# A later place for the exp(k)·v product in the planned order, and a shorter sum-by-sum group at the end of a single block's output product

## The chip, the cores and the metric

The kernel runs on one core of a Trainium2 chip, as one launch. The metric is the device time of the whole program in microseconds (us). TensorE (PE) multiplies, VectorE (DVE) and ScalarE (ACT) do the elementwise work, GpSimd (POOL) helps a little, and SyncE (SP) issues nearly all DMAs. Each engine works through its own instructions in program order; an instruction that waits holds up those behind it on the same engine.

## The reference, cut to what matters

A linear attention feeds two gated expert layers.

```python
q_s = softmax(q, axis=feature);  k_s = softmax(k, axis=sequence)
kv  = k_s.T @ v                  # per batch and head, 64 x 64
x   = q_s @ kv                   # 4608 rows x 512
g, val = x @ w_gate, x @ w_val   # 512 -> 1536
y   = (silu(g) * val) @ w_out    # 1536 -> 512
h   = max(y @ w1, y @ w2, y @ w3)  # 512 -> 768
out = h @ w_out2                 # 768 -> 512
```

There are 8 batches of 8 heads with 576 rows each. All is float32; the kernel splits an operand into a high and a low part in a rounded type (`..h`, `..l`, `hhi`, `hlo`) and adds three products for one.

## The kernel before, in words

The 4608 rows are worked in nine pieces of 512, in six blocks: pieces 0, 1 and 2 singly ("single blocks", `plan_one`), then three pairs (`plan`), which use a seven-product scheme for 2x2 pieces (`wino_unit`). A block runs the G and V products (gate and value, 12 features of 128 columns), the O output product over those 12 features (F1), then the W1, W2, W3 products (6 features, F2), and the P output product over those 6.

**One weight product** (`product`, L668) is six matmuls of 512 columns. A single block's `unit` has four of them, a pair's `wino_unit` seven. **One output feature** (`outs`, L684) is twelve matmuls: four sums e = 0..3, one for each 128 columns of the result (for P: rows), each with three matmuls into its own bank `acc0`..`acc3`. Most features run one after the other ("feature by feature"): all four sums of one feature, then the next. The last ones of a block run "sum by sum" (`emajor`): sum 0 over all features of the group, then sum 1, and so on, so that the first banks are finished early and their readers (`y_plain`, which splits y into the operands b11 and b21 of W1, or `rows_out`, which copies the result rows) start before the last bank is done. A feature needs its hidden values (`hhi`, `hlo`, made by ACT at L719 and DVE at L723 from the last gated product) and its weights (`ow`, in three buffers; in blocks 0 and 1 made by ACT at L581 and DVE at L584, later loaded).

**The attention of the rows to come** runs beside this, in three chains of steps: one for k and v (`k_steps`), two for q (`q_steps`). For each batch and half of its heads the k chain loads, takes the maximum (DVE, POOL), subtracts it (L204, L209), takes exp in three pieces on ACT (`k_exp`, L218: two of `k`, one of the rest `kr`), multiplies exp(k) by v on PE (`kv_mm`, L270, 40 short matmuls into `pkv`), scales (L373 to L383) and splits into `kvhi`, `kvlo`. The q chains end in the products x = q·kv (`x_mm`, L433 to L435). The loads of the next k, its rest and v (L140) overwrite buffers that the product reads, and so stand behind it. The two runs of batch 0 stand in a hand-written prologue; fourteen runs go through the chain.

**The order** of all instructions is made before the launch by a planner written in the kernel: a walk over the PE's items with a planned clock (`clock[0]`), a planned calendar for ACT, DVE, POOL and SP (`do`, `gap`), and fixed costs. Each engine then gets its instructions in the order of planned times; on the chip only semaphores hold them to it. A chain step with kind "P" (a PE step) is put in at a slot: ahead of a weight product, when the planned clock has reached the chain's own time:

```python
if ch["steps"] and ch["steps"][0][0] == "P" and ch["t"] <= clock[0]:
```

Single blocks have a slot ahead of every weight product, pairs only ahead of products 0, 1, 5 and 6 of a `wino_unit`; output features have none, but for a pair's O features 6 to 8 of its second half. The exp steps have planned costs of 1.95, 0.65 and 0.42 us:

```python
steps += [("A", (1.95, 0.65, 0.42)[i], lambda c=c, t=t, i=i: k_exp(t, c, i)) for i in range(3)]
```

The 1.95 holds one ACT table load; an exp that follows a Silu has another table to load again, and so has the Silu after it (L704, planned at 0.62).

Of the kernel before, what the change touches and what calls it, by code (L numbers as in the profile page):

```python
# [21 lines left out]
def linear_attention_moe_moe_kernel(  # L22
# [738 lines left out]
    HALF = {"A": 0.42, "D": 0.43, "G": 0.85}  # L761
    ENG = {"D": nc.vector, "G": nc.gpsimd, "A": None}
    DVE_LATE = 1.0
    G_FIRST = False
    LATER = {3: (1, "P", 0), 4: (2, "O", 0)}
    events = []
# [17 lines left out]
    def gap(e, t, dur):  # L784
        b = busy[e]
        i = bisect.bisect_left(b, (t, t))
        if i and b[i - 1][1] > t:
            t = b[i - 1][1]
        while i < len(b) and b[i][0] < t + dur:
            t = max(t, b[i][1])  # L790
            i += 1
        return t, i
# [11 lines left out]
    def best(t, cost, fn, *a, engines="DG", by=0.0):  # L804

        if G_FIRST and not alone[0] and gap("G", t, cost["G"])[0] + cost["G"] < by:
            return do("G", t, cost["G"], fn, *a, nc.gpsimd)
# [5 lines left out]
    def sync(t, fn, *a):  # L813

        return do("S", t, 0.45, fn, *a) - LAT
# [4 lines left out]
    def take(t):  # L820

        i = min((i for i in range(NT_) if spare[i] is not None), key=lambda i: (max(spare[i], t), -spare[i]))
        t, spare[i] = max(t, spare[i]), None
        return t, i
# [96 lines left out]
    def advance(ch):  # L921
        off = 0.45 * (ch is chains[1]) / 1.8
        while ch["steps"] and ch["steps"][0][0] != "P" and (ch["t"] <= clock[0] + LOOK[len(marks) - 1] or ch.get("bank")):
            e, dur, fn = ch["steps"][0]
            if e == "gate":
                if fn not in gates:
                    return
                ch["t"] = max(ch["t"], gates[fn])
            elif e == "there":
                there[fn] = ch["t"]  # L930
            elif e == "bank":
                bank_free[ch["bank"]] = max(bank_free.get(ch["bank"], 0.0), ch["t"])
                ch["bank"] = None
            elif e == "open":
                gates[fn] = ch["t"]
            elif e == "load":
                t = max(ch["t"], ch.get("last", 0.0))
                for a in fn[1]:
                    t = (math.ceil(t / dur - off) + off) * dur
                    t = max(t + 0.01, sync(t, a))  # L940
                ch["last"] = t
                ch["loaded", fn[0]] = t + 4.5
            elif e == "loaded":
                ch["t"] = max(ch["t"], ch["loaded", fn])
            elif e == "B":
                ch["t"] = best(ch["t"], {"D": dur, "G": 2.0 * dur}, fn)
            elif e in ("D+", "D="):
                t, ch["i"] = take(ch["t"])
                ch["t"] = do("D", t, dur, fn, ch["i"])
            else:  # L950
                ch["t"] = do(e[0], ch["t"], dur, fn)
            if e in ("D-", "D="):
                drop(ch["i"], ch["t"])
            if DEBUG:
                log.append((round(clock[0], 1), chains.index(ch), e, round(ch["t"], 1)))
            ch["steps"].pop(0)
# [16 lines left out]
    def k_steps(runs, n_buf):  # L973

        steps = []
        loads = [k_loads(kbuf[n % n_buf], *run) for n, run in enumerate(runs)]

        def load(n, part):
            if n < len(runs):
                steps.append(("load", 1.8 if n == 0 else 1.0, ((n, part), loads[n][4:] if part else loads[n][:4])))  # L980

        load(0, 0)
        load(0, 1)
        for n, (j, hf) in enumerate(runs):
            c, t = {}, kbuf[n % n_buf]
            if j in LATER:
                steps.append(("gate", 0.0, ("later", j)))
            if n_buf == 2:
                load(n + 1, 0)
            steps.append(("loaded", 0.0, (n, 0)))  # L990
            steps.append(("D=", 1.15, lambda i, c=c, t=t: k_max(t, c, i)))
            steps.append(("loaded", 0.0, (n, 1)))
            steps += [("D", 0.42, lambda c=c, t=t: k_max_rest(t, c)), ("G", 1.4, lambda c=c: k_max_all(c))]
            steps += [("B", (1.22, 0.42)[i], lambda e, c=c, t=t, i=i: k_sub(t, c, i, e)) for i in range(2)]
            steps += [("A", (1.95, 0.65, 0.42)[i], lambda c=c, t=t, i=i: k_exp(t, c, i)) for i in range(3)]

            def kv(bank, c=c, t=t):
                for g in range(HP):
                    kv_mm(t, c, g, bank)

            steps.append(("P", 1.25, kv))
            steps += [("D", 1.1, lambda c=c, t=t: kv_scale(t, c)), ("bank", 0.0, None)]
            if n_buf == 1:
                load(n + 1, 0)
            load(n + 1, 1)
            steps += [("gate", 0.0, ("x", j - 2, hf))] * (j > 2) + [
                ("A", 0.6, lambda c=c, j=j, hf=hf: kv_hi(c, j, hf)),
                ("D", 0.4, lambda c=c, j=j, hf=hf: kv_lo(c, j, hf)),
            ]
            steps.append(("open", 0.0, ("kv", j, hf)))  # L1010
        return steps
# [63 lines left out]
    def conv_job(use, i):  # L1075
# [7 lines left out]
        a0, a1 = gap("A", t, 1.34)[0] + 1.34, gap("A", t, 0.68)[0] + 0.68  # L1083
        dve = gap("D", a1 + LAT, 1.81)[0] + 1.81 + DVE_LATE < gap("D", a0 + LAT, 1.39)[0] + 1.39
        t = do("A", t, 0.68 if dve else 1.34, conv_act, i, dve, o)
# [426 lines left out]
    for n, kinds, out_ in ((F1, ("G", "V"), "O"), (F2, ("W1", "W2", "W3"), "P")):  # L1512
        for p in range(n // 2):
            for i, kind in enumerate(kinds):
                flow.append((kind, p))
                f = 2 * p - 2 + i
# [69 lines left out]
    def plan_one(s):  # L1586

        how = ("conv", "plain")[s] if s < 2 else "parts"
        pair = s + 1 < NS and len(BLOCKS[s + 1]) == 2

        def start():
            if s == 0:
                chains[:] = [{"t": clock[0], "steps": []} for _ in range(3)]
                gates["kv", 0, 0] = gates["kv", 0, 1] = 0.0
                next_k(1)
            have["home"] = clock[0]
            if s == 0:
                gates["rows",] = clock[0]
                at(clock[0], new_rows)
            if s < 2:  # L1600
                at(clock[0], own_qt)

        mark(start)
        n = 0
        if pair:
            x = [lambda n=n: x_wino(n) for n in range(7)]
        for kind, f in flow:
            for j, when in LATER.items():
                if when == (s, kind, f):
                    mark(lambda j=j: gates.__setitem__(("later", j), clock[0]))  # L1610
            if kind in "OP":
                nf = F1 if kind == "O" else F2
                if f < nf - 3:
                    outs(s, kind, [f], 0, nf, how)
                elif f == nf - 3:
                    outs(s, kind, list(range(f, nf)), 0, nf, how, True, {nf - 1: ("s01", "s11")} if s > 1 else None, done=y_plain(0) if kind == "O" else rows_out(BLOCKS[s][0]))
                if (kind, f) == ("P", F2 - 4) and s + 1 < NS:
                    for i in (4, 5, 6) if pair else ():
                        mark(x[i])
                continue  # L1620
            if (kind, f) == ("G", 1) and s + 1 < NS:
                mark(lambda: begin_x(s + 1))
            if s == 0 and (kind, f) in (("G", 0), ("V", 0)):
                unit(0, kind, f, (0,), "conv", (1,), ("b0", "b0", "b2", "b2") if kind == "G" else ("b1", "b1", "b3", "b3"))
            else:
                b = [("b0", "b2", "b1")[(n + i) % 3] for i in range(2)]
                unit(s, kind, f, (0,), how, (0, 1), (b[0], b[0], b[1], b[1]), (kind, f) == ("W1", 0))
                n += 2
            if (s, kind) in MADE_IN:
                keys = [(s, kind, f, 0, i) for i in range(2)]  # L1630
                ahead("made", 8.0, made_job, keys, kind, f)
            if f == F2 // 2 - 1 and kind in ("W1", "W2", "W3") and s + 1 < NS:
                if kind == "W1":
                    mark(lambda: after(s))
                    if pair:
                        mark(x[1])
                elif kind == "W2" and pair:
                    mark(x[2])
                    mark(x[3])
                elif kind == "W3":  # L1640
                    if pair:
                        mark(x[0])
                    else:
                        mark(lambda: x_plain(BLOCKS[s + 1][0], 0))
                        mark(lambda: x_plain(BLOCKS[s + 1][0], 1))
# [209 lines left out]
```

## Time and profile before

| | |
|---|---|
| median of 3 runs | 1601.89 us (1601.54 to 1603.42) |
| the profiled execution's own time | 1603.53 us |
| its span, first to last instruction | 1601.7 us |
| PE busy | 1494.6 us, 93% of the span |
| DVE busy | 1035.5 us, 65% |
| ACT busy | 684.7 us, 43% |
| mean granted PE clock | 0.974 |
| chain that ended last: PE | 74% of the span |

The span is what the profiler saw between the first and the last instruction. A row of waits names who waited, for whom, the total in us, how often, and the longest. A row of a timeline gives start, duration, engine, line, operation and tiles, and in brackets the idle time ahead of it and what ended it. A row of windows gives a stretch, its length, then for each engine busy us and instruction count, then the granted PE clock (1.00 is full speed, 0.50 half).

### The profile page before, as it was taken

What the parts mean: (1) busy time and instruction counts of PE and PEld (TensorE: products, weight loads), DVE (VectorE), ACT (ScalarE), POOL (GpSimd) and SP (SyncE); (2) the same over time, 40 slices, a digit from 0 to 9 for tenths busy, and PEclk for the clock granted to TensorE, in tenths of its full rate; (3) what the DMA queues carried; (4) which work ended last, traced back from release to release, by engine and by line L of the source; (5) the groups of instructions that cost most, each with busy time, mean ns of one, the idle gap of its engine ahead of it and who ended that gap; (6) DMA issues with size and microseconds to landing.
All of it is one profiled execution on the core that took longest, in us unless ns stands there. A gap on an engine that the chain in (4) does not pass through costs nothing.

```text
span 1601.7 us, 20645 instructions
## 1 busy us (share of the span) xinstructions
PE 1494.6 (93%) x6946; PEld 1212.5 (76%) x6946; DVE 1035.5 (65%) x1789; ACT 684.7 (43%) x1184; POOL 98.2 (6%) x86
## 2 busy tenths in 40 slices
PE   3988899899999998989999999999999999999999
PEld 2666777688787886877777877888878878887787
DVE  7879985576867566566549885464388754444643
ACT  3778664643456435453453335432332342224212
POOL 1000000000000001002012130000010200000000
PEclk9999999899999998999999999999999999999999
DMA  6799685866687697886567757875666576646664
GB/s 184 205 316 288 191 238 159 234 196 187 179 268 253 230 321 228 254 247 203 170 214 236 233 178 249 229 207 161 223 181 184 175 233 195 202 139 218 202 187 161
DMA packets 302024, 342.71 MB, mean 214 GB/s; under 512 B 157536, under 2 KB 181088, under 8 KB 301920
## 3 DMA queue, kind: packets, MB, share of 16 engines
q1 hardware_dynamic: 297120, 340.22, 69.1%
q10 hardware_dynamic: 4800, 1.18, 0.4%
q8 instruction: 56, 0.92, 0.2%
q14 instruction: 48, 0.39, 0.1%
HBM read 257.16 MB, written 84.15 MB: 213 GB/s over the span
## 4 chain that ended last, share of the span: by engine, by line
PE 74%; DVE 9%; ACT 6%; DMA 5%; issue 3%; SPq 2%; POOL 0%; DVEq 0%; ACTq 0%; POOLq 0%
PE pb L668 48%; PE pacc L684 15%; PE pb L684 8%; PE pkv L270 1%; DMA ow<-parts_O 1%; DVE tall L738 1%; ACT L704 1%; SPq L156 1%; DVE hlo L723 1%; DMA v_sb<-in_v_dram 1%; ACT L218 1%; PE px L433 1%; DMA wino_G<-wall 1%; ACT plain L527 1%; ACT s L704 1%
## 5 line engine op out<-in xcount | busy, mean ns | idle before, releaser
L738 DVE TENSOR_TENSOR tall<-tall,pb 128x512 f32<-128x512 f32 x234 | 159.5, 683 | 192.2 <-PE pb L668 188.8
L668 PE MATMUL pb<-b11h,wall 128*128 128x512 f32 x756 | 271.6, 401 | 11.1 <-ACT s L704 6.2
L668 PE MATMUL pb<-b21h,wall 128*128 128x512 f32 x756 | 265.2, 393 | 0.0
L684 PE MATMUL pacc<-hhi,ow 128*128 128x512 f32 x576 | 192.8, 398 | 8.4 <-ACT hhi L719 7.2
L668 PEld LDWEIGHTS pb<-b11h,wall 128*128 128x128 f32 x756 | 144.4, 191 | 46.8 <-ACT s L704 8.0
L668 PEld LDWEIGHTS pb<-b21h,wall 128*128 128x128 f32 x756 | 143.3, 190 | 30.4 <-ACT tall L728 0.4
L728 ACT COPY tall<-pb 128x512 f32<-128x512 f32 x112 | 65.7, 587 | 215.1 <-PE pb L668 214.9
L668 PE MATMUL pb<-b11l,wall 128*128 128x512 f32 x378 | 150.1, 397 | 0.9 <-DVE b11l L455 0.9
L668 PE MATMUL pb<-b21l,wall 128*128 128x512 f32 x378 | 148.4, 393 | 1.0 <-DVE b21l L455 1.0
L684 PEld LDWEIGHTS pacc<-hhi,ow 128*128 128x128 f32 x576 | 110.3, 192 | 34.9 <-ACT hhi L719 9.4
L719 ACT CAST hhi<-tall 128x512 fp32r<-128x512 f32 x108 | 66.6, 618 | 150.3 <-DVE tall L713 111.1
L684 PE MATMUL pacc<-hlo,ow 128*128 128x512 f32 x288 | 114.7, 398 | 7.3 <-DVE hlo L723 7.3
L567 DVE TENSOR_TENSOR wall<-plain,wall 128x512 fp32r<-128x512 f32 x126 | 86.1, 686 | 36.2 <-ACT wall L564 36.0
L723 DVE TENSOR_TENSOR hlo<-tall,hhi 128x512 fp32r<-128x512 f32 x104 | 73.6, 708 | 46.3 <-ACT hhi L719 45.8
L684 PE MATMUL pacc<-ow,hhi 128*128 128x512 f32 x288 | 93.4, 406 | 6.5 <-DVE ow L584 6.1
L564 ACT CAST wall<-plain 128x512 fp32r<-128x512 f32 x126 | 76.8, 617 | 51.3 <-PE pb L668 16.2
L684 PE MATMUL pb<-hhi,ow 128*128 128x512 f32 x288 | 91.3, 392 | 1.4 <-DMA ow<-parts_O 1.3
L668 PE MATMUL pb<-t4h,wall 128*128 128x512 f32 x252 | 89.3, 395 | 2.9 <-issue 1.9
L668 PE MATMUL pb<-t3h,wall 128*128 128x512 f32 x252 | 88.6, 392 | 2.0 <-DVE tall L738 1.2
L668 PE MATMUL pb<-t1h,wall 128*128 128x512 f32 x252 | 89.9, 398 | 0.0
L668 PE MATMUL pb<-b22h,wall 128*128 128x512 f32 x252 | 88.3, 391 | 0.0
L668 PE MATMUL pb<-t2h,wall 128*128 128x512 f32 x252 | 88.0, 390 | 0.0
(231 smaller groups left out, 2773.5 us busy)
## 6 DMA issues: line engine op xcount, KB each, us to landing
ow<-parts_O SPq DMA_DIRECT2D x77, 512.0 KB, 4.5
wall<-wino_W SPq DMA_DIRECT2D x153, 256.0 KB, 3.1
wall<-wino_G SPq DMA_DIRECT2D x102, 256.0 KB, 3.1
wall<-wino_V SPq DMA_DIRECT2D x102, 256.0 KB, 3.2
ow<-parts_P SPq DMA_DIRECT2D x32, 512.0 KB, 5.5
wino_W<-wall SPq DMA_DIRECT2D x63, 256.0 KB, 3.8
wino_G<-wall SPq DMA_DIRECT2D x42, 256.0 KB, 3.0
wino_V<-wall SPq DMA_DIRECT2D x42, 256.0 KB, 3.8
```

The costliest lines, as they stand in the source:

```text
L156: return [lambda p=p, g=g, n=n, i=i: nc.sync.dma_start(out=t["qp"][p, g, n], in_=i) for p, g, n, i in todo]
L218: nc.scalar.activation(out=a, in_=a, func=AF.Exp)
L270: nc.tensor.matmul(out=c["pkv"][u * D:(u + 1) * D, g, :], lhsT=lhsT, rhs=rhs, start=i == 0, stop=i == R,)
L564: nc.scalar.copy(out=wall[:, i:i + 2, 0], in_=plain[kind, f].rearrange("p (a n) -> p a n", a=2))
L567: eng.tensor_tensor(out=wall[:, i:i + 2, 1], in0=plain[kind, f].rearrange("p (a n) -> p a n", a=2), in1=wall[:, i:i + 2, 0], op=ALU.subtract,)
L668: nc.tensor.matmul(out=banks[bank], lhsT=a, rhs=b, start=start and n == 0, stop=stop and n == 5, skip_group_check=True,)
L684: nc.tensor.matmul(out=banks[bank], lhsT=lhsT, rhs=rhs, start=first and n == 0, stop=last and n == 2)
L704: nc.scalar.activation(out=s, in_=a(), func=AF.Silu)
L719: nc.scalar.copy(out=hid[key][0], in_=st["h", key[1], key[2], key[3]])
L723: eng.tensor_tensor(out=lo, in0=st.pop(("h", key[1], key[2], key[3])), in1=hi, op=ALU.subtract)
L728: nc.scalar.copy(out=tall[:, i], in_=banks[bank])
L738: eng.tensor_tensor(out=out_, in0=tall[:, x], in1=banks[bank] if isinstance(bank, str) else tall[:, bank], op=ALU.add)
```

## The change

The k chain gets a new kind of step, "wait", which moves only the chain's planned time, by 3.0 us; it stands between the exps and the product. It makes no instruction. And in `plan_one`, for O and P alike, the sum-by-sum group begins at feature nf - 2 and not at nf - 3: feature nf - 3 runs feature by feature, like the ones ahead of it.

```diff
+    KV_WAIT = 3.0
...
             elif e == "bank":
                 bank_free[ch["bank"]] = max(bank_free.get(ch["bank"], 0.0), ch["t"])
                 ch["bank"] = None
+            elif e == "wait":
+                ch["t"] += dur
...
-            steps.append(("P", 1.25, kv))
+            steps += [("wait", KV_WAIT, None), ("P", 1.25, kv)]
...
                 nf = F1 if kind == "O" else F2
-                if f < nf - 3:
+                if f < nf - 2:
                     outs(s, kind, [f], 0, nf, how)
-                elif f == nf - 3:
+                elif f == nf - 2:
                     outs(s, kind, list(range(f, nf)), 0, nf, how, True, ...
```

## Rows read from the trace of the kernel before

**Rows 1.** The page's busy times: engine, us, share of the span, instructions.
```profile
PE 1494.6 (93%) x6946; PEld 1212.5 (76%) x6946; DVE 1035.5 (65%) x1789; ACT 684.7 (43%) x1184; POOL 98.2 (6%) x86
```

**Rows 2.** Waits of PE: who, for whom, us in total, times, longest.
```profile
PE pkv L270 <- ACT kr_sb L218: 16.7, 6, 4.0
...
PE pkv L270 <- ACT k L218: 3.1, 1, 3.1
...
PE px L433 <- ACT kvhi L392: 0.6, 1, 0.6
PE pkv L270 <- ACT k_sb L218: 0.3, 1, 0.3
```

**Rows 3.** Windows: a kv product without a wait, then the six with one.
```profile
117.97:119.28 1.31, 1.31 (x41) 1.24 (x40) 1.28 (x4) 0.79 (x2) 0.00 (x0) 1.00 0.67 171
258.59:261.06 2.47, 1.53 (x41) 1.33 (x41) 0.36 (x1) 2.46 (x4) 0.00 (x0) 1.00 0.03 7
289.97:305.53 15.56, 9.02 (x59) 7.27 (x59) 6.93 (x16) 10.42 (x16) 0.00 (x0) 0.67 0.76 207
484.68:490.51 5.83, 4.41 (x53) 3.69 (x53) 4.42 (x7) 3.34 (x6) 0.00 (x0) 1.00 0.88 284
687.82:704.99 17.17, 12.86 (x84) 10.65 (x83) 7.58 (x18) 9.18 (x18) 0.00 (x0) 0.90 0.67 185
728.26:739.62 11.36, 8.23 (x59) 6.99 (x59) 8.98 (x20) 4.41 (x11) 5.64 (x5) 0.70 0.79 240
776.43:792.95 16.52, 12.77 (x83) 10.45 (x83) 8.47 (x16) 8.18 (x14) 1.30 (x1) 0.90 0.36 87
```

**Rows 4.** The chain that ended last: one output feature and seven products, undisturbed.
```profile
1036.84 9.52 PE pb L668 x42
1046.36 2.72 PE pacc L684 x12
```

**Rows 5.** ACT's timeline ahead of and behind the wait that ends at 693.04.
```profile
683.51 1.28 ACT L704 ACT_TABLE_LOAD   x1
...
690.65 0.62 ACT L704 ACTIVATE s<-tall 128x512 f32<-128x512 f32 x1
691.28 1.28 ACT L218 ACT_TABLE_LOAD   x1
692.57 0.42 ACT L218 ACTIVATE kr_sb<-kr_sb 64x256 f32<-64x256 f32 x1
692.89 0.60 ACT L719 CAST hhi<-tall 128x512 fp32r<-128x512 f32 x1
```

**Rows 6.** Waits of SP's queue for the kv product.
```profile
SPq L140 <- PE pkv L270: 32.4, 7, 10.9
```

**Rows 7.** Windows of 48 matmuls: the last four features of O or P.
```profile
147.55:171.82 24.27, 14.49 (x49) 10.23 (x48) 22.45 (x43) 10.03 (x19) 1.35 (x1) 0.79 0.68 221
234.25:250.33 16.08, 13.24 (x49) 10.11 (x48) 12.06 (x22) 6.05 (x11) 1.06 (x1) 0.89 0.48 149
...
423.06:440.83 17.77, 14.00 (x50) 10.66 (x48) 12.73 (x22) 7.72 (x14) 1.36 (x1) 0.81 0.98 300
...
607.17:622.33 15.16, 12.92 (x49) 10.00 (x48) 12.62 (x23) 7.47 (x15) 0.65 (x1) 0.89 0.85 259
```

**Rows 8.** PE's timeline: waits within those windows.
```profile
241.64 0.49 PE L684 MATMUL pacc<-ow,hhi 128*128 128x512 f32 x1 [2.73 <-DVE ow L584]
...
431.57 0.79 PE L684 MATMUL pacc<-ow,hhi 128*128 128x512 f32 x1 [3.33 <-DVE ow L584]
```

**Rows 9.** PE's timeline: the first W1 products behind block 0's O.
```profile
173.78 0.50 PE L668 MATMUL pb<-b11l,wall 128*128 128x512 f32 x1 [0.90 <-DVE b11l L455]
```

**Rows 10.** SP's timeline: first and last of the 16 q loads behind the run at 776.43.
```profile
781.36 0.33 SPq L156 DMA_DIRECT2D k_sb<-in_q_dram  x1
...
813.43 0.42 SPq L156 DMA_DIRECT2D k_sb<-in_q_dram  x1
```

**Rows 11.** PE's timeline: the x product that needs these loads.
```profile
885.05 0.28 PE L433 MATMUL px<-qthi,kvhi 128*128 128x256 f32 x1
```

## The prediction, made before the changed kernel was run

> **What bounds the kernel now.** I read the page's busy times first: PE is busy 93% of the span [rows 1], so the kernel is PE's stream of matmuls, and what can be won is where that stream stands still or runs slowly: 1601.7 - 1494.6 = 107 us idle, and the half-clock stretches inside the busy time. The table of PE's waits comes next, to see who makes PE wait. What stands out is the product of exp(k) and v: 16.7 + 3.1 + 0.3 = 20.1 us, in eight waits, for an exp of the chain [rows 2]. Then I went along PE's timeline and cut a window round each of these places: six of the fourteen products wait (two of them twice), and the reader is to compare each window with the undisturbed one of 1.31 us [rows 3]. Last, the ends of the single blocks' output products, cut in the same way, 48 matmuls each [rows 7].
>
> **Part 1, the later product: what it can remove.** Undisturbed, one weight product is 9.52 / 7 = 1.36 us and one output feature 2.72 us [rows 4]. Taking these and 1.31 us for the product itself off the windows [rows 3]: 2.47 - 1.31 = 1.16; 15.56 - 1.31 - 3 x 1.36 = 10.17; 5.83 - 1.31 - 2 x 1.36 = 1.80; 17.17 - 1.31 - 9.52 = 6.34; 11.36 - 1.31 - 1.36 - 2.72 = 5.97; 16.52 - 1.31 - 9.52 = 5.69. Together 31.1 us, of which 20.1 are the waits (a window's length less its busy PE: 0.94, 6.54, 1.42, 4.31, 3.13 and 3.75) and 11.0 slow clock: the granted clock is 0.67, 0.90, 0.70 and 0.90 in the four windows with the longest waits, and 1.00 in the undisturbed one. So a wait there costs half as much again as it lasts.
>
> **Why the exp is late, and whether 3.0 us is enough.** The planner charges one table load to a run's first exp and none to the exps and Silus that alternate behind it. Ahead of the exp that ends the wait at 692.99 ACT loads a table four times that way, of which the first and the last are shown, 1.28 us each [rows 5]: 5.1 us that the plan lacks, against 4.3 us waited. So planned slack at that product was small, at most about 1 us, and the same pattern (four loads) stands in the windows at 289.97 and 776.43. A planned 3.0 us alone would cover 3 of 6.5, 4.3 and 3.75 us; but a product goes only into a slot, and the step to the next one is what counts. At 687.82 and 776.43 it stands ahead of product 0 of a seven-product unit; product 1 is 1.36 us on and too early, so it moves ahead of product 5, 5 x 1.36 = 6.8 us. At 289.97 three weight products of the unit are left, the last slot 2.72 us on, and then a feature without slots: 3 x 1.36 + 2.72 = 6.8 us. At 731.39 it is ahead of product 6, and the next slot is 1.36 + 2.72 = 4.1 us on; at 484.68 it is 2 x 1.36 + 2.72 = 5.4 us; at 258.59 2.7 to 4.1 us. Each step is longer than the wait that it has to cover (6.5, 4.3, 3.75, 3.1, 1.4, 0.9). If the planned slack lets the nearer slot do, 2.72 at 289.97 and 1.36 at the two seven-product units, 3.8 + 2.9 + 2.4 = 9 us of waits stay.
>
> The Trainium skill (ScalarE: Activation LUTs, "What ACT_TABLE_LOAD costs") gives 1283 ns for the load and about 1380 ns more for a drain, 2.66 us for each switch. The trace agrees on the load; of a drain it shows nothing: the Silu ahead ends at 690.65 + 0.62 = 691.27, the load starts at 691.28 and the exp at 692.57 [rows 5]. By the page's price four switches would be 10.6 us of lateness, 3 to 4 us past the step of 6.8 at three places, and the gain some 10 us smaller; the row decides.
>
> **What it adds and moves.** No instruction is added. Later with the product come its scale, `kvhi` and `kvlo`, and the x product that reads them; PE has waited for `kvhi` 0.6 us in all [rows 2], so these have room. In the SP queue the loads of the next k, rest and v stand behind the product and wait for it 32.4 us in seven places already [rows 6]; they move with it in the planned order, so nothing else is stuck for longer, but every following run of the same chain starts later, by 3 to 7 us each time. In the first pair, with four runs on one buffer, this adds up: I expect the last, now at 776.43, to lose its place in the G and V units, which end at 792.95, and to go to the O features 6 to 8 of the second half, some 30 us later; the second q loads, which wait for it, go there too. POOL's part of the chain (a reduction for each run) keeps its place within the chain; POOL is busy 6% [rows 1].
>
> **What is late next.** PE no longer waits, and so meets ACT's lateness elsewhere: behind the exp at 692.57 comes a cast to 693.49 [rows 5] and only then the copy that frees the bank of product 0, to about 694.1; product 4 wants that bank at 687.82 + 4 x 1.36 = 693.3. That is 0.8 us of a new wait; at 776.43 the same sum gives none. For the new phases of the later runs I have no row: between 0 and the eight waits over again (20 us); I take two waits of an average place, 2 x 3 us, as ACT is idle again soon after each exp. Part 1: 31.1 - 0.8 - 6 = 24 us gained, with ends 5 and 31.
>
> **Part 2, the shorter group.** Four features are 4 x 2.72 = 10.9 us. The windows show 16.08, 17.77 and 15.16 us for the three P ends, losses of 5.2, 6.9 and 4.3, and 24.27 us for block 0's O [rows 7]. Now the last two features start after 12 + 12 matmuls and not after 12 + 3: nine matmuls, 9 x 2.72 / 12 = 2.04 us later, while what makes their operands stays where it is. The waits are at the last feature's first weights, 2.73 and 3.33 us at P of blocks 0 and 1 [rows 8]; they shrink to 0.7 and 1.3, and part of the slow clock that follows them (0.89, 0.81 in the windows) goes too. With all of it 12 us; I take 7, as the plan may put the waited-for splits later as well, with ends 0 and 12. Block 0's O is another thing: DVE is busy 22.45 of 24.27 us [rows 7], so the operands come when DVE gets to them, and the W1 product behind it waits for DVE again [rows 9]. The 2 us won there wait at W1: nothing. On the other side, the banks now finish 2 x 0.68 = 1.36 us apart, not 2.04, so the operand b11 of W1 is ready that much later against PE: at most 1.36 us in each of three O ends, 4.1 in all; between nothing and that I take 1 us lost, as only block 0's W1 has waited there. Part 2: 6 us gained, ends -4 (slower) and 14.
>
> **The sum.** 24 + 6 = 30 us off the profiled execution's 1603.53 gives 1573.5; the median of the runs is 1.6 us below it, so 1572, rounded up to 1573.
>
> **The rivals.** (a) ACT's lateness is passed on: it had to do the same loads, and PE waits for Silu, casts or banks in place of exp. For it: in the window at 289.97 ACT is busy 10.42 of 15.56 us [rows 3]. Against: the work that PE now does first was prepared before. With half of part 1 and part 2, 12 + 3 = 15 us: 1587. (b) It hardly moves: a planned slack of 3 us or more, where the wait changes nothing. The same rows speak against it, the waits being nearly as long as the loads that the plan lacks. Then part 2 alone, 1603.5 - 6 - 1.6 = 1596. (c) The slower side: the k chain of the first pair, 3 to 7 us later at each of four runs, ends so late that its q loads and the x products miss their block, and PE stands empty before the next one. The q run's loads took 32 us after the product, from 781.4 to 813.8 [rows 10], and its x product stands at 885 [rows 11]; so it decides only if the product comes later than about 845, past the O slots. Then some 30 us of idle and 15 at half clock: 1572 + 45 = 1617. Against: the O slots are there, and the chain has exps done by then.
>
> **Chances.** Forecast 0.63, its own range 1562 to 1583; (a) 0.22; (b) 0.07; (c) 0.08. A measurement can tell about 0.2%, 3 us, from no change. The forecast, (a) and most of (b) are faster; a part of (b), with part 2 at its poor end, is the same: faster 0.88, same 0.04, slower 0.08. The range reaches through (a) to (b): 1560 to 1596.
>
> **What would show it.** Right: PE's waits for L218 fall from 20 us to below 5; the granted clock in the windows round the products is 1.00; the product stands ahead of product 5 where it stood ahead of product 0; the P ends of blocks 0 to 2 take 11 to 14 us; the last run of the first pair stands among the O features. Wrong: waits of PE for Silu (L704) or `hhi` (L719) that grow by as much as those for exp shrink, which is (a); products in their old places, (b); a PE gap ahead of the P ends of the first pair, (c).

## The result, and the profile after

The changed kernel takes 1566.42 us (median of 4 runs, 1561.44 to 1568.43) beside 1601.97 us for the kernel before: ratio 0.9772, 95% interval [0.9747, 0.9797]; the medians lie 35.6 us apart. The profiled execution takes 1565.22 us, its span is 1563.2 us, 38.5 us shorter than before's. The mean granted clock rose from 0.974 to 0.986.

The page's busy times of the changed kernel (engine, us, share, instructions), beside [rows 1]:

```profile
PE 1480.0 (95%) x6946; PEld 1201.1 (77%) x6946; DVE 1032.7 (66%) x1787; ACT 682.1 (44%) x1184; POOL 100.6 (6%) x86
```

The same 6946 matmuls are busy for 14.6 us less, which is slow clock that went, and the idle time fell from 107 to 83 us. From PE's waits after the change, for comparison with [rows 2]:

```profile
PE pacc L684 <- DVE hlo L723: 6.9, 8, 2.3
PE pacc L684 <- ACT hhi L719: 6.0, 3, 3.2
PE pb L668 <- POOL wall L638: 6.0, 1, 6.0
PE pb L668 <- ACT s L704: 4.6, 3, 1.9
...
PE pacc L684 <- DVE ow L584: 3.5, 3, 1.4
...
PE pkv L270 <- DVE tall L738: 2.1, 2, 1.9
```

No wait for L218 is left: the 20.1 us for the chain's exp are gone. One new wait stands out, 6.0 us for a POOL instruction; and two kv products now wait for L738 of VectorE, 2.1 us in all. The windows of the changed kernel: the six kv products that answer, run by run, to the waiting ones of [rows 3], among them the stretch of the POOL wait (692.03), and last a product that did not wait before (length, PE, PEld, DVE, ACT, POOL, clock, DMA):

```profile
255.41:256.72 1.31, 1.31 (x41) 1.24 (x40) 1.15 (x2) 0.00 (x0) 0.00 (x0) 1.00 0.53 131
296.39:297.70 1.31, 1.31 (x41) 1.24 (x40) 1.24 (x6) 1.29 (x3) 0.00 (x0) 1.00 0.93 309
483.27:484.59 1.32, 1.32 (x41) 1.25 (x41) 1.32 (x3) 0.50 (x1) 0.00 (x0) 1.00 0.00 0
660.66:661.98 1.32, 1.32 (x42) 1.25 (x41) 1.28 (x3) 0.00 (x0) 0.00 (x0) 1.00 0.91 217
692.03:709.47 17.44, 11.42 (x43) 9.01 (x42) 7.17 (x13) 5.63 (x11) 4.91 (x4) 0.80 0.41 139
719.17:720.76 1.59, 1.32 (x41) 1.25 (x41) 1.56 (x4) 0.00 (x0) 0.00 (x0) 1.00 0.86 310
777.14:778.46 1.32, 1.32 (x42) 1.25 (x41) 0.56 (x1) 0.62 (x1) 0.00 (x0) 1.00 0.90 264
612.35:615.53 3.18, 1.31 (x40) 1.28 (x40) 3.01 (x6) 0.37 (x2) 0.00 (x0) 1.00 0.93 252
```

Five of the six products run through in 1.31 or 1.32 us at full clock; the one at 719.44 waits 0.27 us for L738. The product at 614.22 answers to one that did not wait before (645.54): it waits 1.87 us for L738, at full clock. The fifth row is a unit of seven products without a kv product: 17.44 us for what takes 9.52 undisturbed, 7.9 us lost. What it waited for shows on POOL's timeline (start, us, engine, line; in brackets the idle time before):

```profile
695.85 1.08 POOL L195 PARTITION_ALL_REDUCE kb<-km  x1 [9.67 <-PE pb L668]
704.70 0.71 POOL L638 TENSOR_TENSOR wall<-twos,wall 128x256 fp32r<-128x256 f32 x1 [7.77 <-issue]
705.39 1.91 POOL L256 TENSOR_TENSOR q_sb<-q_sb,qs 128x1024 f32<-128x1024 f32 x1
```

POOL ends its reduction at 696.93 and starts the low part of a weight at 704.70; in the 7.77 us between it waits for nothing that the records show. PE's row for it:

```profile
705.47 0.80 PE L668 MATMUL pb<-b22h,wall 128*128 128x512 f32 x1 [6.02 <-POOL wall L638]
```

The ends of O in block 0 and of P in blocks 0 to 2, beside [rows 7]:

```profile
230.09:243.07 12.98, 11.46 (x49) 8.93 (x48) 10.74 (x20) 6.06 (x11) 1.06 (x1) 1.00 0.55 142
403.68:416.45 12.77, 11.44 (x49) 8.93 (x48) 10.29 (x19) 7.96 (x16) 0.00 (x0) 1.00 0.81 241
581.70:593.25 11.55, 11.22 (x50) 8.93 (x48) 10.80 (x19) 6.75 (x14) 0.00 (x0) 1.00 0.96 297
146.13:168.29 22.16, 14.78 (x49) 10.50 (x48) 21.66 (x43) 10.48 (x19) 1.35 (x1) 0.77 0.75 249
```

The three P ends lost 3.1 + 5.0 + 3.6 = 11.7 us of their 49.0, and the slow clock in them is gone; block 0's O lost 2.1. So the 38.5 us of the span come out as -31.1 (kv windows), -11.7 (P ends), -2.1 (block 0's O), -3.6 (the first units of the first pair, told below), +7.9 (the POOL wait), which is -40.6; elsewhere 2.1 us net were lost, and the first pair's O features alone lost 2.6 (44.26 - 1.31 us for what took 40.32).

### The profile page after: what moved, and what is told of

It is laid out like the page before. It is cut to its first block, busy times and chain, and to the rows that moved or that the text cites. A ratio compares the mean times of both kernels' runs of the same rounds, so it can differ in the third digit from the quotient of the medians.

```text
span 1563.2 us, 20625 instructions
## 1 busy us (share of the span) xinstructions
PE 1480.0 (95%) x6946; PEld 1201.1 (77%) x6946; DVE 1032.7 (66%) x1787; ACT 682.1 (44%) x1184; POOL 100.6 (6%) x86
## 4 chain that ended last, share of the span: by engine, by line
PE 76%; DVE 11%; DMA 6%; issue 3%; ACT 3%; SPq 1%; POOL 0%; DVEq 0%; ACTq 0%
PE pb L668 51%; PE pacc L684 15%; PE pb L684 8%; DMA v_sb<-in_v_dram 1%; PE pkv L270 1%; DMA plain<-raw_V 1%; DVE stage L543 1%; DVE tall L738 1%; DVE hlo L723 1%; DVE wall L567 1%; DMA raw_O<-plain 1%; SPq L156 1%; PE px L434 1%; DMA out_dram<-tall 1%; PE px L433 1%
## 5 line engine op out<-in xcount | busy, mean ns | idle before, releaser
L738 DVE TENSOR_TENSOR tall<-tall,pb 128x512 f32<-128x512 f32 x234 | 159.4, 683 | 195.1 <-PE pb L668 182.8
L668 PE MATMUL pb<-b11h,wall 128*128 128x512 f32 x756 | 267.1, 394 | 8.1 <-ACT s L704 4.6
L668 PE MATMUL pb<-b21h,wall 128*128 128x512 f32 x756 | 263.0, 390 | 0.0
L684 PE MATMUL pacc<-hhi,ow 128*128 128x512 f32 x576 | 191.8, 396 | 7.3 <-ACT hhi L719 6.0
L668 PEld LDWEIGHTS pb<-b11h,wall 128*128 128x128 f32 x756 | 142.3, 189 | 42.4 <-ACT s L704 5.9
L668 PEld LDWEIGHTS pb<-b21h,wall 128*128 128x128 f32 x756 | 141.9, 188 | 30.0 <-ACT tall L728 0.4
L668 PE MATMUL pb<-b11l,wall 128*128 128x512 f32 x378 | 147.9, 391 | 0.5 <-DVE b11l L455 0.5
L668 PE MATMUL pb<-b21l,wall 128*128 128x512 f32 x378 | 147.4, 390 | 0.4 <-DVE b21l L455 0.4
L684 PEld LDWEIGHTS pacc<-hhi,ow 128*128 128x128 f32 x576 | 110.0, 191 | 33.3 <-ACT hhi L719 8.6
L684 PE MATMUL pacc<-hlo,ow 128*128 128x512 f32 x288 | 114.7, 398 | 6.6 <-DVE hlo L723 6.6
L668 PE MATMUL pb<-b22h,wall 128*128 128x512 f32 x252 | 90.3, 399 | 7.0 <-POOL wall L638 6.0
L684 PE MATMUL pb<-hhi,ow 128*128 128x512 f32 x288 | 91.1, 391 | 1.1 <-DMA ow<-parts_O 0.9
L684 PE MATMUL pacc<-ow,hhi 128*128 128x512 f32 x288 | 89.3, 390 | 2.6 <-DVE ow L584 2.6
L668 PE MATMUL pb<-t4h,wall 128*128 128x512 f32 x252 | 88.7, 393 | 1.9 <-issue 1.9
L668 PE MATMUL pb<-t3h,wall 128*128 128x512 f32 x252 | 88.4, 391 | 2.1 <-DVE tall L738 1.2
L668 PE MATMUL pb<-t1h,wall 128*128 128x512 f32 x252 | 88.8, 393 | 0.0
L668 PE MATMUL pb<-t2h,wall 128*128 128x512 f32 x252 | 88.1, 390 | 0.0
```

The lines of the kernel that those rows point to most:

```text
L668: nc.tensor.matmul(out=banks[bank], lhsT=a, rhs=b, start=start and n == 0, stop=stop and n == 5, skip_group_check=True,)
L684: nc.tensor.matmul(out=banks[bank], lhsT=lhsT, rhs=rhs, start=first and n == 0, stop=last and n == 2)
L738: eng.tensor_tensor(out=out_, in0=tall[:, x], in1=banks[bank] if isinstance(bank, str) else tall[:, bank], op=ALU.add)
```

## The experiments

Each is compared with the kernel before on the same chip, and each ratio has its 95% interval. Gains in us are worked out from these ratios; by its ratio the change itself gains 36.5 us.

**The wait alone.**

```diff
-                if f < nf - 2:
+                if f < nf - 3:
...
-                elif f == nf - 2:
+                elif f == nf - 3:
```

> Part 1 alone: the planned wait of 3.0 us, the output groups of three as before. My theory (the waits for exp are simply covered): PE's waits of L270 for L218 are below 2 us, and against the kernel before it wins the 31 us of the six windows, less the one new wait seen after the change (6 us for a POOL instruction, some 8 with its slow clock): about 1578, ratio 0.985. Rival (lateness of ACT is passed on): waits for L218 fall, but those for L704, L719 and L564 grow by 10 us or more: about 1590, ratio 0.993. Rival (the shorter group did most of it): ratio above 0.993 with no growth of other waits.

Measured: 1576.82 us, ratio 0.9846 [0.9820, 0.9871], 24.7 us faster. PE's waits for the chain's exp in this run:

```profile
PE pkv L270 <- ACT kr_sb L218: 1.2, 1, 1.2
```

The wait for Silu is 1.9 us where it was 6.2, so lateness is not passed on there. The planned wait took all but 1.2 us of the exp waits away by itself. No PE wait for POOL stands in this trace, for which I had put down 8 us; other waits grew, for DMAs of `ow` from 1.6 to 6.2 us and for L738 ahead of weight and kv products from 2.2 to 7.3. That the time still came out as expected is in part luck. The P ends, left in threes, still gained 3.6 us from the shift of the chain: 16.09, 15.47 and 13.88 us.

```profile
234.85:250.94 16.09, 13.25 (x49) 10.07 (x48) 12.39 (x22) 6.75 (x13) 1.06 (x1) 0.89 0.45 144
413.89:429.36 15.47, 13.00 (x50) 9.90 (x49) 11.23 (x21) 7.47 (x15) 1.06 (x1) 0.89 0.90 246
592.75:606.63 13.88, 11.30 (x50) 8.86 (x48) 12.69 (x23) 7.60 (x15) 0.71 (x1) 1.00 0.84 267
```

**The shorter group alone.**

```diff
-    KV_WAIT = 3.0
+    KV_WAIT = 0.0
```

> Part 2 alone: planned wait 0.0, the shorter groups. My theory: the three P ends of the single blocks lose some 12 us against before (16.1, 17.8, 15.2 us become about 13, 13, 11.5), block 0's O 2 us; the exp waits stay near 20 us. About 1588, ratio 0.991. Rival (W1 pays it back, its operands being ready later): ratio 0.997 or more, with waits for L455 above 4 us. Rival (the two parts do not add: the P ends won only because the chain moved): P ends as before, ratio 1.0.

Measured: 1583.07 us, ratio 0.9891 [0.9872, 0.9911], 17.5 us faster. The P ends are 13.01, 15.18 and 11.53 us, 9.3 us less than before, so they do win by themselves. But the exp waits did not stay, which I had expected:

```profile
PE pkv L270 <- ACT kr_sb L218: 6.5, 4, 3.2
PE pkv L270 <- issue: 4.4, 1, 4.4
PE pkv L270 <- ACT k L218: 0.8, 1, 0.8
```

7.3 us carry the exp's name where it was 20.1, though no wait was planned. The 4.4 us without a releaser end at 633.81, 2.05 us behind the run's last exp but only 0.10 us behind L738 of VectorE, for which the same run's product waits in the changed kernel:

```profile
631.35 0.41 ACT L218 ACTIVATE kr_sb<-kr_sb 64x256 f32<-64x256 f32 x1
632.43 1.28 DVE L738 TENSOR_TENSOR tall<-tall,pb 128x512 f32<-128x512 f32 x2
```

So that wait most likely ended with L738. The shorter plan of the O and P ends shifts the chain (the product that stood at 179.87 stands at 191.76), and exps and Silus meet in another way; that this is what the other 12.8 us were is argued, not shown. The two parts thus take away the same waits. Their gains alone add to 42 us beside 36.5 together, a difference no larger than its noise. The waits that it also removes are a good part of why the second alone is worth three times what I gave it.

**A planned wait of 0.5 us.**

```diff
-    KV_WAIT = 3.0
+    KV_WAIT = 0.5
```

> The change with a planned wait of 0.5 us in place of 3.0. My theory (the product goes to the next slot, and its distance counts): a product whose planned slack is below 0.5 goes one slot on, 1.36 us at the places at 289.97, 687.82 and 776.43 of the kernel before, and the others stay; so waits for L218 stay at 12 to 17 us and the time is between the two, 1580 to 1588, ratio 0.987 to 0.991. Rival (any small change of order breaks the coincidence that makes exp late): waits for L218 below 5 us and the time near 1566, ratio 0.978.

Measured: 1581.98 us, ratio 0.9888 [0.9868, 0.9907]: no better than none. The exp waits are 5.2 + 0.2 us, below the 12 I expected, and much as in the run with no wait (6.5 + 0.8); 4.7 us more have no releaser in the records and end, as there, 0.1 us behind L738. So neither expectation was met as it stood: the time is in the range of the first, the exp waits are not. A planned wait of 0.5 us adds nothing to the shorter group, and the low number has the same cause as there.

**A planned wait of 6.0 us.**

```diff
-    KV_WAIT = 3.0
+    KV_WAIT = 6.0
```

> The change with a planned wait of 6.0 us in place of 3.0. My theory: the exps are covered at 3.0 already, so more wait covers nothing; waits for L218 stay at nothing, and the time is within 8 us of the change, ratio 0.972 to 0.983, any difference coming from other engines' order. Rival (c of the prediction: the chain gets so late that x products miss their place): new waits of PE ahead of x products (L433, L434 for kvhi or kvlo) of 10 us or more, ratio 0.985 or more.

Measured: 1564.30 us, ratio 0.9767 [0.9750, 0.9783], the same as with 3.0. No wait for L218 is left either; PE waits once for `kvhi`, 2.8 us ahead of an x product. 3.0 us had covered the exps, and the x products stand twice the delay. The equal time hides other differences: PE's wait for POOL's L638 is 1.7 us here where it was 6.0.

**Copy in place of Silu, in the kernel before.**

```diff
-            nc.scalar.activation(out=s, in_=a(), func=AF.Silu)
+            nc.scalar.activation(out=s, in_=a(), func=AF.Copy)
```

> The kernel before, with Copy in place of Silu at L704 (the gate's function is left out), so that exp and Silu no longer alternate tables on ACT; order and shapes are those of before. My theory (table loads that the plan does not charge make the exps late): loads at L704 vanish, those at L218 fall from 23 to one or two; PE's waits for L218 fall from 20.1 us to 3 to 6, the one left being the place at 731.39, where POOL's subtraction is late; some 25 us faster than before, ratio 0.984. Rival (the subtraction, or ACT's other work, makes exp late): waits for L218 above 12 us, ratio above 0.992.

Measured: 1573.77 us, ratio 0.9838 [0.9815, 0.9861], 26 us faster with before's order; this kernel leaves out the gate's function. ACT's groups of table loads, first of the kernel before, then of this run (line, count, total us, mean ns):

```profile
L704 ACT ACT_TABLE_LOAD x32 | 41.1, 1283 | 18.9 <-PE pb L668 18.4
L218 ACT ACT_TABLE_LOAD x23 | 29.5, 1283 | 0.4
L243 ACT ACT_TABLE_LOAD x8 | 10.3, 1283 | 0.1
```

```profile
L319 ACT ACT_TABLE_LOAD x1 | 1.3, 1283 | 12.9 <-DMA w<-in_v_dram 12.9
```

One load, in the prologue (L319), is left of 64, and PE's waits for the exp fall to 3.3 us in two places:

```profile
PE pkv L270 <- ACT kr_sb L218: 3.3, 2, 2.7
```

2.7 us of that is the place that was at 731.39, behind POOL's subtraction. So in before's own order the table loads made about five sixths of the exp waits. The run takes away the loads that the plan charges too; that the uncharged ones matter is for the next run. Part of the 26 us is not from these waits: ACT is busy 602.9 us where it was 684.7, and everything else that it makes comes earlier too.

**Charging the loads in the plan, in place of the wait.**

```diff
-    KV_WAIT = 3.0
+    KV_WAIT = 0.0
...
-(1.95, 0.65, 0.42)[i]
+(1.95, 1.95, 1.72)[i]
```

> The change with no planned wait, but with the exps' planned costs raised by one table load each for the second and third (1.95, 1.95, 1.72), shorter groups kept. My theory: the plan then knows the lateness, the product moves by about as much as with the wait, waits for L218 below 4 us, time within 8 us of the change, ratio 0.973 to 0.983. Rival (the wait works because it moves the product alone, while dearer exps push ACT's other work about): waits for L218 small but others larger, no better than the shorter group alone, ratio 0.989 or more.

Measured: 1571.22 us, ratio 0.9824 [0.9802, 0.9845]. The waits for L218 are gone entirely, as with the wait; the time lies 0.5% above the change's, and the intervals just miss each other (0.9797 and 0.9802). PE's other waits in this run hold 2.0 us for `kvhi` and 3.2 us for `hhi` in the P and O features of pairs, for which the changed kernel waits 0 and 0.8. Charging the cause that was named is enough to remove the exp waits; a bare wait on the product is no worse a remedy than the truth in the plan.

**A made weight's low part kept off POOL.**

```diff
-best(t, HALF, wino_lo, key, k, by=use - 1.5)
+best(t, HALF, wino_lo, key, k, by=use - 1.5, engines="D")
```

> The change, with the low part of a made weight (L638, wino_lo) kept off POOL. After the change PE waits 6.0 us once for such a POOL instruction, which starts 7.8 us after POOL's reduction with nothing that it waits for in the records. My theory: POOL needs that time between the reduction and an instruction of another kind, so without it on POOL the wait goes, with its slow clock: 8 us faster than the change, about 1558, ratio to before 0.973. Rival (DVE is then as late, being loaded with these): PE waits as long for DVE L638, about 1566, ratio 0.978.

Measured: 1557.10 us, ratio 0.9727 [0.9707, 0.9746], 7 us faster than the change by the ratios. PE's unit of seven where the new wait was is undisturbed, with a kv product in it (9.52 + 1.31 us are 10.83):

```profile
693.51:704.57 11.06, 11.06 (x84) 9.05 (x82) 8.98 (x23) 5.10 (x11) 1.92 (x1) 1.00 0.80 238
```

The chain moved too, that product by some 76 matmuls, so this run alone does not part the two causes; in the next one the kv products of this stretch stand close to where the change has them.

**No elementwise work on POOL.** POOL keeps its reductions and nothing else of the plan.

```diff
-        if alone[0]:
-            engines = engines.replace("G", "")
+        engines = engines.replace("G", "")
```

> The change with all elementwise work that the planner may give to POOL kept on DVE; POOL keeps its reductions. In the traces POOL stands 7 to 10 us between a reduction and an elementwise instruction, in either order. My theory: those gaps are what made the one new wait of 6.0 us, so without them the time is that of the run with L638 off POOL or better, 1548 to 1558, ratio 0.967 to 0.973. Rival (DVE takes over some 75 us of work and the pairs' operand splits get late): PE's waits for DVE grow by 10 us or more, 1562 or slower.

Measured: 1549.23 us, ratio 0.9684 [0.9661, 0.9707], 14 us faster than the change by the ratios. PE waits for nothing between 640 and 740 us. DVE takes the work over for 6 us of busy time more, and POOL is left with 24 us:

```profile
PE 1477.0 (95%) x6946; PEld 1203.5 (78%) x6946; DVE 1038.9 (67%) x1839; ACT 674.7 (44%) x1177; POOL 23.8 (2%) x35
```

**The same edit on the kernel before.**

> The kernel before, with the elementwise work that the planner may give to POOL kept on DVE. My theory: POOL's 7 to 8 us between the reduction and the subtraction made two of before's waits, 3.1 us for exp at 731.39 and 3.7 us for Silu (behind an exp on ACT) at 635.73; these two go, the other exp waits (17 us in places without POOL) stay at 10 us or more; 8 to 15 us faster than before, ratio 0.991 to 0.995. Rival (POOL's gaps were hidden before): ratio 0.997 or more. Rival (POOL's work made most exp waits): waits for L218 below 5 us.

Measured: 1579.72 us, ratio 0.9877 [0.9852, 0.9902], 20 us faster, more than the 8 to 15 expected. The exp waits are 14.1 us:

```profile
PE pkv L270 <- ACT kr_sb L218: 10.4, 5, 3.6
...
PE pkv L270 <- ACT k L218: 3.7, 1, 3.7
```

The place at 731.39 no longer waits, those at 260, 293, 487 (without POOL near) do much as before, 0.9, 7.3 and 1.4 us beside 0.9, 6.5 and 1.4. So two lacks of the plan, table loads and POOL's gaps, stood behind the exp waits, the loads behind most. The exp waits fell by 6.0 us, and PE's waits for Silu (6.2 us before) are gone; the rest of the 20 us I have not taken apart.

**P's last feature alone as the group.**

```diff
+                last = nf - (2 if kind == "O" else 1)
-                if f < nf - 2:
+                if f < last:
...
-                elif f == nf - 2:
+                elif f == last:
```

> The change, with P's last feature alone as its sum-by-sum group (all features one after the other), O as in the change. My theory (each feature taken out of the group gives the last one nine, here six, more matmuls of time): the P ends of blocks 0 to 2, now 13.0, 12.8 and 11.6 us, lose what they have above 10.9: 3 to 4.5 us faster than the change, ratio 0.9745 to 0.9755. Rival (the waited-for splits stand behind something that moves with them, or the four row copies now crowd at the end): P ends as in the change, ratio 0.977 or more.

Measured: 1560.26 us, ratio 0.9758 [0.9737, 0.9778]; the time alone does not part it from the change. The P ends do:

```profile
230.66:241.59 10.93, 10.93 (x50) 8.94 (x48) 9.66 (x18) 6.55 (x12) 0.00 (x0) 1.00 0.49 131
402.19:414.31 12.12, 11.46 (x50) 8.93 (x48) 10.19 (x19) 7.20 (x13) 0.17 (x1) 1.00 0.95 277
577.49:588.37 10.88, 10.88 (x50) 9.02 (x48) 10.22 (x18) 5.99 (x12) 0.00 (x0) 1.00 0.83 263
```

33.9 us for three ends where the change has 37.3 and the floor is 3 x 10.88 = 32.6. Six matmuls more of time for the last feature took most of what was left, as nine had taken most before; block 1 keeps 1.2 us.

**Both edits that helped.** No elementwise work on POOL, and P's last feature alone, on top of the change.

> The change, with both edits that helped: no elementwise work on POOL, and P's last feature alone as its group. My theory: they touch different places, so the gains add: 17 us from the first, 4 to 6 from the second, about 1543, ratio 0.963 to 0.967. Rival (the DVE load that POOL leaves behind makes the P ends late again): ratio 0.968 or more.

Measured: 1539.68 us, ratio 0.9615 [0.9597, 0.9633]: 25 us faster than the change and 62 us faster than before, the best version here. That is below the 0.963 that I expected: alone the two gain 14 and 2 us on the change. The 9 us that they gain beyond the sum lie barely outside the noise, and no run shows where they come from.

## Why the prediction was right

**The rate and the exp waits.** The kernel was taken as PE's stream with holes, 31.1 us of them round the kv products. At the six places all but 0.27 us of it went, waits and slow clock alike. Alone this part gave 24.7 us, for which I had 24; what it lost elsewhere was not what I had reckoned with.

**Why exp is late.** The uncharged table loads were the right cause for most of it, as Copy in place of Silu and the charged loads show. I named no other. At 731.39 it was POOL: its subtraction starts 7.6 us after the reduction, and exp waits for it, with no table load between the run's exps:

```profile
728.79 0.63 ACT L218 ACTIVATE k_sb<-k_sb 128x512 f32<-128x512 f32 x1 [5.88 <-POOL k_sb L204]
```

The forecast did not need this, as the step that it gave there, 4.1 us, was longer than the wait anyway.

POOL's subtraction also bears on 3.6 us that I did not forecast: before, PE waited 3.71 us for a Silu at 635.73 that stood on ACT behind an exp that waited for POOL.

```profile
621.68 1.13 POOL L195 PARTITION_ALL_REDUCE kb<-km  x1 [114.32 <-DVE km L191]
629.90 2.38 POOL L204 TENSOR_TENSOR k_sb<-k_sb,kb 128x1024 f32<-128x1024 f32 x1 [7.09 <-PE pb L668]
632.31 0.63 ACT L218 ACTIVATE k_sb<-k_sb 128x512 f32<-128x512 f32 x1 [6.94 <-POOL k_sb L204]
635.73 0.79 PE L668 MATMUL pb<-b11h,wall 128*128 128x512 f32 x1 [3.71 <-ACT s L704]
```

After the change the same order falls differently against the G unit, and that stretch (622.33 to 659.23, then 593.25 to 626.57) is 36.9 - 33.3 = 3.6 us shorter, the new 1.87 us at 614.22 included.

**Where the product goes.** The step to the next slot, not the 3.0 us, was to decide. At the unit that had it ahead of product 0 (687.82) it now stands behind 30 of the unit's matmuls, ahead of product 5 (660.66), as worked out; four table loads still stand among the run's exps and Silus, and the last exp ends 3.9 us ahead of the product:

```profile
656.34 0.42 ACT L218 ACTIVATE kr_sb<-kr_sb 64x256 f32<-64x256 f32 x1
```

The first pair's last run is at 777.14, between matmuls of the O features of the second half, as worked out too. With 0.5 us nothing was won, with 6.0 no more than with 3.0.

At other places the working was wrong and the outcome in part luck. Counted in matmuls of L668 and L684 ahead of them, the products that stood at 289.97, 484.68 and 731.39 stand some 67, 94 and 99 later, or 15, 21 and 22 us at 9.52 / 42 us each, where the forecast had one slot, 4 to 7 us: delays added up from run to run, and the shorter group moves the chain too. At 296.39 and 777.14 no load stands between the run's exps any more (289.04 to 292.58, 757.71 to 759.69). With the wait alone the product that stood at 687.82 stands some 20 matmuls earlier and does not wait, as its exps follow one load (649.66) and not four. So part of the waits went because exps and Silus no longer alternate, which I did not forecast; how large a part, no run tells.

**What is late next.** I took 0.8 us for a bank and 6 us for places without a row; the POOL wait with its slow clock is 7.9 us, and 2.1 us more are for L738. That the size is close is luck, as the place was not seen: an instruction on POOL that stands behind a reduction in its queue. I passed over POOL as 6% busy, and its gaps are not in its busy time.

**The shorter group.** This is the term that was mis-sized. I had 12 us in the P ends if all of it came, took 7 of it, none in block 0's O and 1 us lost at W1, 6 in all; measured are 11.7 in the P ends and 2.1 in O, and W1's wait behind O fell too, from 1.9 to 0.9 us. The waits at the last feature's first weights, for which I had 0.7 and 1.3 us left, are 1.41 and 1.23:

```profile
238.02 0.49 PE L684 MATMUL pacc<-ow,hhi 128*128 128x512 f32 x1 [1.41 <-DVE ow L584]
411.41 0.50 PE L684 MATMUL pacc<-ow,hhi 128*128 128x512 f32 x1 [1.23 <-DVE ow L584]
```

Measured from the start of the window, the waited-for splits moved by less than 1 us (0.5 later in block 0, 0.8 earlier in block 1), so my fear that the plan would put them later hardly came true. By itself the part gave 17.5 us, past my upper end of 14; 9.3 us of that are the P ends, and it moved the chain too.

**The rivals.** Lateness passed on to Silu, casts and banks: PE's waits for Silu are 4.6 us where they were 6.2, for `hhi` ahead of `pacc` 6.0 where they were 7.6, for L738 in all 4.4 where they were 4.7; it did not happen. That the wait hardly moves the product is refuted by its places. The slower case, a chain too late for its x products, did not come even with 6.0 us.

## What to carry to other kernels

Where a plan orders in-order queues by fixed costs, look in the trace for an engine that waits always on the same step, and ask which cost the plan lacks there. Here a planned wait ahead of the consumer and the missing cost put into the plan both removed those waits. Either also moves everything behind it, so look at the new order, and not only at the place. Price such a wait by the window round it, not by its idle time: here 20 us of waits were 31. And an engine with a small busy share can still hold others up by the gaps between its instructions.

## What the runs showed of the hardware

POOL stands at least 6.7 us between a partition reduction and an elementwise instruction, in either order, with no instruction in the gap. In the traces of the two kernels the shortest such gaps are 6.69 to 9.92 us, some with no reason in the records; in all ten traces that have such pairs the shortest is 6.68. It is 7.77 us after the reduction at 695.85 of the changed kernel, and in the kernel before 8.73 us ahead of one and 7.62 us behind the next:

```profile
670.72 0.74 POOL L638 TENSOR_TENSOR wall<-twos,wall 128x256 fp32r<-128x256 f32 x1 [37.75 <-ACT wall L634]
680.19 1.08 POOL L195 PARTITION_ALL_REDUCE kb<-km  x1 [8.73 <-issue]
717.66 1.10 POOL L195 PARTITION_ALL_REDUCE kb<-km  x1 [36.39 <-DVE km L191]
726.39 2.38 POOL L204 TENSOR_TENSOR k_sb<-k_sb,kb 128x1024 f32<-128x1024 f32 x1 [7.62 <-PE pb L668]
```

Two elementwise instructions can stand back to back (704.70 and 705.39 above). The Trainium skill (GPSIMD Engine Reference, "2.1 Instruction dispatch") says that the first call of a freshly loaded POOL kernel pays about 6 us with nothing visible in a profile. The gaps here have that form and are longer by 1 to 4 us; that it is this load is argued, not shown. Shown is that keeping elementwise work off POOL took 20 us off the kernel before and 14 us off the changed one.
